# Moving three conversion steps behind a unit boundary, dropping a scatter's wait for a fill, and shifting the first batch's means by a step

## The chip, the cores and the metric

The kernel runs on one core of a Trainium2 chip. The metric is the device time of one launch in microseconds (us). The core has five engines with instruction streams of their own: TensorE (PE, whose weight loads are listed as PEld), VectorE (DVE), ScalarE (ACT), GpSimd (POOL) and SyncE (SP), which in this kernel issues nearly all DMA transfers. Each engine works through its stream strictly in order, and an instruction that waits for a semaphore holds back everything behind it on its engine.

## The reference

Three layers follow one another; every tensor is float32 for the kernel's purposes except the last layer's two weights, which arrive as 64-bit floats.

```python
# attention: 2 batches x 8 heads, S=768, D=64, block=32, window=16
k_sum = k.reshape(B, H, nb, block, D).max(axis=3)
v_sum = v.reshape(B, H, nb, block, D).mean(axis=3)
scores_l = where(|i-j| < window, scale * q @ k.T, -1e9)      # local
scores_s = scale * q @ k_sum.T + log(block)                  # 24 block keys
a = softmax(concat([scores_l, scores_s]));  out = a @ concat([v, v_sum])
# top-1 mixture of experts: 1536 tokens, 512 wide, 8 experts, hidden 1024, capacity 384
expert = argmax(x @ w_gate); gate = softmax prob of it
disp[e, pos] = x[i]          # the first `capacity` tokens of each expert
y = relu(disp @ w1[e]) @ w2[e];  out[i] = gate * y[expert, pos]
# dense layer: 512 -> 2048 -> 512
h = x @ w_in;  g = where(h > 0, h, exp(min(h, 0)) - 1);  return g @ w_out
```

## The kernel before

**Attention** (lines 455 to 775) goes in 24 steps `n` (12 query tiles of 128 tokens, two head groups each). Each step makes scores on PE (`stage_s`, L615), the row maximum on DVE (`stage_max`, L627), exponentials on ACT (`stage_exp`, L640), and, some steps later, transposes (`stage_t`, L661, copied out by ACT at L666) and the product with the values (`stage_o`, L675, scaled by DVE at L686). The order is written out by hand: `T_AT`, `O_AT`, the lists `EARLY`, `LATE`, `END`, and a function `late(n)` that adds the loads and side jobs of step `n`.

The block means of the values are made for each batch of 768 tokens: `pair_sum(b, m)` adds two halves of a value tile in place (L567; there are three tiles, m = 0 to 2, held in `w2raw_131`, `133` and `135`), `block_means` multiplies by a constant averaging matrix on PE (L572), all into one bank of PSUM, and `put_first`, `keep_means` and `put_means` copy the 24 rows of means to where the value tiles of the steps expect them (DVE L589, ACT L590 and L577, POOL L580). `put_spread` (L455) writes a constant into half of a query buffer, once per buffer.

**Dispatch.** Each finished token tile is routed (`gate_1` to `gate_6`, L703 to L764: logits, argmax, the token's position in its expert). POOL then scatters the tile's 128 rows to the DRAM table `xdisp` with an indirect DMA (`put`, L775). The table has a region for each expert, and at its end, from `E * REG` on, a region where no token goes; at step 21 SP writes a constant row into that region (`fill`, L904, 128 x 3 rows of 514 numbers). The scatters are declared free of one another by a no-dependence group called "put"; the list `puts` holds them, and the next load of rows (`load_rows`, L216) waits for all in it.

**Units.** The experts' work runs in units of 384 rows. A unit has eight hidden slices `f` of 128: first layer L241, ReLU on ACT (L1269, `hh` L1270), the low part `hl` on DVE (L1271), second layer L275, three slices later (LAG = 3). Every float32 product is made as three products of a high and a low part. ACT makes the high parts of the weights (`wah`, `wbh`, L233 and L286) and DVE the low parts (`wal` L234, `wbl` L287), in slices `c` of 256. `split_x` (part of `prologue(j, 1)`) transposes the unit's rows on PE (L255), then ACT takes the high part `xh` (L256) and DVE the low part `xl` (L257), four pieces each. With these inputs three units run; the first is mixed into the tail of attention.

**Conversions.** The dense layer's weights come as pairs of 128 x 512 blocks of 64-bit floats, and DVE turns each pair to float32 in three steps (L419, L422, L412). The raw pairs go through a ring of two buffers (`raw_160`, `raw_161`). The last step of a pair issues, on SP, the load of the pair two places later (`conv_next`, L378, two transfers of 512 KB). Units 1 and 2 convert five pairs each, 15 steps spread over the slices f = 0 to 6 by `convert_some`. Unit 1's fifth pair is pair 18 (to `wout_108` from `raw_160`), and its end releases the load of pair 22 into the same buffer; unit 2 converts pairs 20, 22, 24, 26 and 28.

At f = 3 and f = 6 of a unit SP also loads the next unit's weights (`NEXT`: three transfers, then four; an eighth, `w2raw_137`, goes at the next unit's start), 512 KB each. A unit starts with that load, `prologue` (unit 2's row split), the store of the unit's identifiers (L1183) and the load of the rows of the unit after it. After the units the dense layer runs in three groups of 512 rows (L1383).

Of the kernel before, what the change touches and what calls it, by code (L numbers as in the profile page):

```python
# [26 lines left out]
E, F = 8, 1024  # L27
FF = 2048
P = 128
# [9 lines left out]
REG = NT + SLOT  # L39
# [55 lines left out]
def moe_chain_kernel(  # L95
# [339 lines left out]
    with ExitStack() as att:  # L435
# [17 lines left out]
        def put_spread(n, g, copy):  # L453
            rows = heads(1 - g)
            copy(QS[n][rows, g], C("spread")[rows].unsqueeze(1).to_broadcast([D, KD, P]))  # L455
# [132 lines left out]
        def put_first(n):  # L588
            nc.vector.tensor_copy(VXS[n][WK:NK, 0, :], VP[WK:NK, :])  # L589
            nc.scalar.copy(VXS[n][WK:NK, 1, :], VP[WK:NK, :])  # L590

        MEANS_AT = ({2: [1], 3: [2], 4: [3]}, {13: [(2, 0)], 14: [(2, 1)], 15: [(3, 0)], 16: [(3, 1)]})

        OPS = BANK[4].rearrange("p (g u d) -> p g u d", g=2, u=4)
        GPS = BANK[6][:, 0:256].rearrange("p (g n) -> p g n", g=2)
# [73 lines left out]
        def stage_o(i, g):  # L669
            es = st.pop(("t", i, g))  # L670
            vx = vx_of(i)
            op = OPS[:, g]
            for u in range(4):
                for j in range(2):
                    nc.tensor.matmul(  # L675
                        op[j * TQ : (j + 1) * TQ, u, :],
                        es[:, u, j * TQ : (j + 1) * TQ],
                        vx[:, j, (2 * u + g) * D : (2 * u + g + 1) * D],
                        start=True,
                        stop=True,  # L680
                    )
            if g:
                xts[i] = a3.tile([P, ROW], F32, tag="xr", name="xr", bufs=6)
                xt = xts[i][:, 0:DM].rearrange("p (u g d) -> p g u d", g=2, d=D)
                rd = st.pop(("rd", i))
                nc.vector.tensor_tensor(xt, OPS, rd.to_broadcast([P, 2, 4, D]), op=ALU.mult)  # L686
                fill_in()
# [185 lines left out]
        def late(n):  # L873
# [15 lines left out]
                nc.vector.memset(ones_f, 1.0)  # L889
            if n == 1:  # L890
                for g in range(2):
                    put_spread(2, g, nc.gpsimd.tensor_copy)
                nc.gpsimd.memset(fill_row, 0.0)
            if n == 3:
                nc.gpsimd.tensor_copy(fill_row[:, DM:], C("oob")[:, 0:2])
# [5 lines left out]
                load_k(1, 0 if n == 1 else 2, 2)  # L901
            if n == 21:
                nc.sync.dma_start(ids.rearrange("(p a) o -> p (a o)", a=REG // P), oobs)
                nc.sync.dma_start(xdisp[E * REG :, :].rearrange("(s p) d -> p s d", p=P), fill)  # L904
            if n == 0:
                load_q(2)
            if n % 2 == 1 and (n + 5) // 2 < NTT:
# [74 lines left out]
        for n in range(NST - 1):  # L982
            at = lambda lag: steps[n - lag] if 0 <= n - lag < NST else None
            stage_s(*at(0))
            if n == 3:
                stage_o(0, 0)
            for m in T_AT.get(n, ()):
                stage_t(*steps[m])
                stage_e(*steps[m])
            for gate, i in EARLY.get(n, ()):  # L990
                gate(i)
            if at(2) and at(2)[1]:
                st["early"] = early_o(at(2)[0])
            stage_max(*at(0))
            stage_exp(*at(0))
            if n == 2:
                for m in (1, 2):
                    block_means(0, m, 0, last=(m == 2))
            if n == 2:
                put_first(0)  # L1000
                keep_means()
            for slot in MEANS_AT[0].get(n, ()):
                put_means(slot)
            if n == 1:
                block_means(0, 0, 0, first=True)
                block_means(0, 0, 1)
                stage_t(*at(1))
                stage_e(*at(1))
                for m in (1, 2):
                    pair_sum(0, m, nc.vector)  # L1010
            for m in O_AT.get(n, ()):
                stage_o(*steps[m])
            for gate, i in LATE.get(n, []) + END.get(n, []):
                gate(i)
            late(n)
# [154 lines left out]
    def convert_some(j, f):  # L1170

        if j < len(CONV_UNIT):
            n = (CONVS[j + 1] - CONVS[j]) // 2
            todo = [step for m in range(n) for step in conversion(ORDER[CONVS[j] // 2 + m])]
            lo, hi = (min(m, NF1 - 1) * len(todo) // (NF1 - 1) for m in (f, f + 1))
            for step in todo[lo:hi]:
                step()

    def expert_of(j, queue=nc.sync):
        return queue.value_load(listed(0, j), min_val=0, max_val=E - 1)  # L1180
# [67 lines left out]
    def unit(j, expert, finish):  # L1248

        if j > 1:  # L1250
            load_w(expert, NEXT[2])
            for n in range(j == 2, 2):
                prologue(j, n)
        base = nc.sync.value_load(listed(2, j), min_val=0, max_val=NT)
        if j + 1 < MAXU:
            branch_ahead(f"units{j}", n_units > j + 1)
# [55 lines left out]
    def units(j, expert, finish):  # L1312
        if j:
            expert, finish = unit(j, expert, finish)
        if j + 1 < MAXU:
            with tc.If(n_units > j + 1, label=f"units{j}") as more:
                units(j + 1, expert, finish)
            with more.Else():
                if j:
                    last_parts()  # L1320
                if j + 1 < len(CONV_UNIT):
                    for n in range(CONVS[j + 1], NCHUNK - CONV_LATE, 2):
                        convert(ORDER[n // 2])
        else:
            last_parts()
# [228 lines left out]
```

## Time and profile before

| what | value |
|---|---|
| three runs | 420.69, 422.80, 423.19 us (median 422.8) |
| profiled execution | 421.81 us, of it span 419.7 us |
| PE busy | 398.4 us (95% of the span) |
| DVE busy | 336.1 us (80%) |
| ACT busy | 234.7 us (56%) |
| POOL busy | 64.8 us (15%) |
| DMA | 63.60 MB, mean 152 GB/s |
| granted clock of TensorE, mean | 0.993 of full speed |

The profiled execution took 421.81 us, 2.1 us more than its span, and lies 1.0 us under the median of the three runs. Busy shares are means over stages with different limits, so the argument reads stretches of the trace: about 0 to 95 us is attention with the first unit's loads, 95 to 112 us the end of routing, 112 to 210 us the units, and then the dense layer. In a row of the timeline the bracket gives the time that the engine stood idle just before the instruction and what released it.

### The profile page before, as it was taken

The page shows a single profiled execution, that of the slowest core. Times are in us where ns is not written, and L with a number is a line of the kernel's source. Part 1 is how long each engine was busy: PE and PEld are TensorE (multiplying, and loading weights), DVE is VectorE, ACT ScalarE, POOL GpSimd, SP SyncE. Part 2 cuts the span into 40 slices and gives each one's busy share as a digit, 9 for nine tenths or more (in the row PEclk, how much of TensorE's full clock was granted, in tenths as well). Part 3 has the DMA queues.
Part 4 walks back from the last instruction along what each step waited for, and adds up shares of the span by engine and source line. Part 5 has one row for each costly group of instructions (what it writes and reads, how often), then busy time and mean ns, then how long its engine had stood idle before and what let it go on. Part 6 is the DMA issues. An engine that isn't in the chain of part 4 may idle for free.

```text
span 419.7 us, 7891 instructions
## 1 busy us (share of the span) xinstructions
PE 398.4 (95%) x2736; PEld 349.1 (83%) x2736; DVE 336.1 (80%) x675; ACT 234.7 (56%) x586; POOL 64.8 (15%) x129
## 2 busy tenths in 40 slices
PE   7999999989999999799999999999999999999994
PEld 4577677667898989799989889998989898989883
DVE  6789787686589988788879999997788777778870
ACT  4687697762565737166497578645343435343421
POOL 5334776515300000000000000002000002000002
PEclk9999999999999999899999999999999999999998
DMA  8999999699476786985577000202000200100002
GB/s 245 256 285 263 270 275 280 188 345 364 155 228 226 244 301 232 332 255 209 171 271 274 0 2 1 77 0 77 0 0 2 76 2 35 40 2 0 2 2 77
DMA packets 33691, 63.60 MB, mean 152 GB/s; under 512 B 5302, under 2 KB 16191, under 8 KB 33642
## 3 DMA queue, kind: packets, MB, share of 16 engines
q1 hardware_dynamic: 31962, 58.28, 44.9%
q0 software_dynamic: 1680, 4.73, 3.1%
q8 instruction: 23, 0.38, 0.4%
q14 instruction: 26, 0.21, 0.1%
HBM read 50.19 MB, written 13.40 MB: 152 GB/s over the span
## 4 chain that ended last, share of the span: by engine, by line
PE 48%; issue 19%; DVE 16%; DMA 7%; ACT 6%; POOL 1%; SPq 1%; DVEq 0%; another core or an unknown queue 0%; ACTq 0%; POOLq 0%
PE bank L241 21%; PE bank L1383 13%; PE bank L275 5%; DMA half<-in_q_dram 3%; PE bank L661 2%; PE bank L615 2%; ACT ex L640 2%; DMA w2raw<-in_v_dram 2%; PE bank L675 2%; DMA rows<-in_k_dram 2%; DMA raw<-in_moe_w_out_dram 1%; DVE wal L234 1%; DVE win L422 1%; DVE win L412 1%; DVE xrow L1445 1%
## 5 line engine op out<-in xcount | busy, mean ns | idle before, releaser
L1383 PE MATMUL bank<-wout_r,hh 128*128 128x512 f32 x144 | 56.6, 393 | 1.0 <-DVE wout_r L1363 1.0
L640 ACT ACTIVATE ex<-bank,nm 128x120 f32<-128x120 f32 x96 | 33.5, 370 | 9.9 <-DVE nm L627 9.9
L1430 ACT ACTIVATE cst<-bank 128x384 f32<-128x384 f32 x24 | 11.8, 490 | 39.2 <-PE bank L241 39.2
L1430 ACT ACTIVATE xrow<-bank 128x384 f32<-128x384 f32 x24 | 11.7, 489 | 38.4 <-PE bank L241 38.2
L1383 PEld LDWEIGHTS bank<-wout_r,hh 128*128 128x128 f32 x144 | 27.1, 188 | 5.9 <-DVE wout_r L1363 1.7
L1395 POOL DMA_INDIRECT out_dram<-ysb,idt x3 | 2.9, 973 | 178.8 <-DVE xrow L1446 178.2
L1383 PE MATMUL bank<-w2raw_r,hl 128*128 128x512 f32 x72 | 28.7, 399 | 0.5 <-DVE hl L1411 0.5
L1383 PE MATMUL bank<-w2raw_r,hh 128*128 128x512 f32 x72 | 28.2, 392 | 0.0
L241 PE MATMUL bank<-yh,win_r 128*128 128x384 f32 x128 | 27.0, 338 | 0.0
L615 PE MATMUL bank<-kw,half 128*64 128x120 f32 x384 | 24.7, 271 | 1.4 <-DMA half<-in_q_dram 1.4
L1395 POOL DMA_INDIRECT out_dram<-raw,idt x6 | 6.1, 1024 | 119.3 <-ACT raw L1392 118.1
L615 PEld LDWEIGHTS bank<-kw,half 128*64 128x64 f32 x384 | 19.7, 136 | 5.7 <-issue 5.1
L241 PE MATMUL bank<-xh,wal 128*128 128x384 f32 x104 | 23.4, 347 | 0.6 <-DVE wal L234 0.6
L241 PEld LDWEIGHTS bank<-yh,win_r 128*128 128x128 f32 x128 | 22.8, 188 | 0.3
L275 PE MATMUL bank<-hh,wbh_r 128*128 128x384 f32 x96 | 21.1, 341 | 0.0
L1445 DVE SCALAR_TENSOR_TENSOR xrow<-xrow 128x384 f32<-128x384 f32 x24 | 13.3, 556 | 9.2 <-ACT xrow L1432 8.5
L640 ACT ACTIVATION_READ_ACCUMULATOR ex<-bank,nm 128x1 f32 x96 | 20.6, 215 | 0.0
L275 PE MATMUL bank<-hl,wbh_r 128*128 128x384 f32 x96 | 20.6, 336 | 0.0
L1445 DVE SCALAR_TENSOR_TENSOR xrow<-cst,xrow 128x384 f32<-128x384 f32 x24 | 13.3, 556 | 8.6 <-ACT cst L1432 8.6
L241 PEld LDWEIGHTS bank<-xh,wal 128*128 128x128 f32 x104 | 18.7, 193 | 1.8 <-DVE wal L234 1.6
L661 PE MATMUL bank<-cst,ex 128*120 128x128 f32 x96 | 17.2, 289 | 0.7 <-ACT ex L640 0.5
L666 ACT COPY es<-bank 120x512 f32<-120x512 f32 x24 | 14.2, 593 | 6.3 <-PE bank L661 4.4
(286 smaller groups left out, 1108.0 us busy)
## 6 DMA issues: line engine op xcount, KB each, us to landing
raw<-in_moe_w_out_dram SPq DMA_DIRECT2D x16, 512.0 KB
w1raw<-in_moe_w_dram SPq DMA_DIRECT2D x12, 512.0 KB
w2raw<-in_moe_w_dram SPq DMA_DIRECT2D x12, 512.0 KB
raw<-in_moe_w_in_dram SPq DMA_DIRECT2D x10, 512.0 KB
half<-in_q_dram SPq DMA_DIRECT2D x24, 128.0 KB
w2raw<-in_v_dram SPq DMA_DIRECT2D x6, 512.0 KB
rows<-in_moe_w_in_dram SPq DMA_DIRECT2D x6, 512.0 KB
yr<-ydT SPq DMA_DIRECT2D x4, 768.0 KB
```

The lines of the kernel that those rows point to most:

```text
L234: nc.vector.tensor_tensor(lo, src, hi.bitcast(F32), op=ALU.subtract)
L241: nc.tensor.matmul(hp, wa[a][:, kk, cols], xa[b][:, kk, :], start=(n == kk == 0), stop=(n == 2 and kk == KD - 1))
L275: nc.tensor.matmul(ACC[d][:, 0:SLOT], wb[a][:, jj, d * P : (d + 1) * P], hb[b], start=(f == 0 and n == 0), stop=(f == NF1 - 1 and n == 2),)
L615: nc.tensor.matmul(sp[cols, u, :], qts[i][:, g, u, cols], kws[i][:, g, u, j, :], start=True, stop=True)
L640: nc.scalar.activation(ex[:, u, :], sp[:, u, :], AF.Exp, bias=nm[:, u : u + 1], accum_out=dens[i][:, g, u])
L661: nc.tensor.transpose(ep[:, u, :], ex[:, u, :], ident)
L666: nc.scalar.copy(es, st.pop(("e", i, g)))
L675: nc.tensor.matmul(op[j * TQ : (j + 1) * TQ, u, :], es[:, u, j * TQ : (j + 1) * TQ], vx[:, j, (2 * u + g) * D : (2 * u + g + 1) * D], star ...
L1383: nc.tensor.matmul(ACC[s], ga[a][:, cols], wb[b][:, jj, :], start=(f == n == 0), stop=(f == NF2 - 1 and n == 2),)
L1395: put = nc.gpsimd.indirect_dma_start(out, bass.IndirectOffsetOnAxis(ap=IDT[g % 3][:, s : s + 1], axis=0), OBS[(NS * g + s) % len(OBS)], No ...
L1430: nc.scalar.activation(x, hp, AF.Relu, scale=-1.0)
L1445: nc.vector.scalar_tensor_tensor(z, x, 1.0, z, op0=ALU.add, op1=ALU.mult)
```

## The change

Four edits. (1) The first batch's last pair sum (tile m = 2) moves on DVE from the end of step 1 to step 2, behind that step's maximum; its PE product moves behind step 3's scores, and the copies of the means (`put_first`, `keep_means`, the `put_means` slots) move a step later; `stage_o(0, 0)` follows them to the end of step 3's exponentials. (2) Two `put_spread` copies at step 1 move from POOL to ACT. (3) The fill's store joins the group "put" and the list `puts`. (4) In unit 1, the conversion steps that stood at f = 6 (the three steps of pair 18) are kept back and issued after unit 2's `prologue`, or in the other branch where there is no unit 2.

```diff
--- before.py
+++ after.py
@@ -589,7 +589,7 @@
             nc.vector.tensor_copy(VXS[n][WK:NK, 0, :], VP[WK:NK, :])
             nc.scalar.copy(VXS[n][WK:NK, 1, :], VP[WK:NK, :])
 
-        MEANS_AT = ({2: [1], 3: [2], 4: [3]}, {13: [(2, 0)], 14: [(2, 1)], 15: [(3, 0)], 16: [(3, 1)]})
+        MEANS_AT = ({3: [1], 4: [2], 5: [3]}, {13: [(2, 0)], 14: [(2, 1)], 15: [(3, 0)], 16: [(3, 1)]})
 
         OPS = BANK[4].rearrange("p (g u d) -> p g u d", g=2, u=4)
         GPS = BANK[6][:, 0:256].rearrange("p (g n) -> p g n", g=2)
@@ -889,7 +889,7 @@
                 nc.vector.memset(ones_f, 1.0)
             if n == 1:
                 for g in range(2):
-                    put_spread(2, g, nc.gpsimd.tensor_copy)
+                    put_spread(2, g, nc.scalar.copy)
                 nc.gpsimd.memset(fill_row, 0.0)
             if n == 3:
                 nc.gpsimd.tensor_copy(fill_row[:, DM:], C("oob")[:, 0:2])
@@ -901,7 +901,10 @@
                 load_k(1, 0 if n == 1 else 2, 2)
             if n == 21:
                 nc.sync.dma_start(ids.rearrange("(p a) o -> p (a o)", a=REG // P), oobs)
-                nc.sync.dma_start(xdisp[E * REG :, :].rearrange("(s p) d -> p s d", p=P), fill)
+                spare = nc.sync.dma_start(xdisp[E * REG :, :].rearrange("(s p) d -> p s d", p=P), fill).ins
+                tc.declare_no_dep(spare, group="put", reason="no token has a row there")
+                tc.add_to_no_dep_group("put", spare)
+                puts.append(spare)
             if n == 0:
                 load_q(2)
             if n % 2 == 1 and (n + 5) // 2 < NTT:
@@ -983,7 +986,7 @@
             at = lambda lag: steps[n - lag] if 0 <= n - lag < NST else None
             stage_s(*at(0))
             if n == 3:
-                stage_o(0, 0)
+                block_means(0, 2, 0, last=True)
             for m in T_AT.get(n, ()):
                 stage_t(*steps[m])
                 stage_e(*steps[m])
@@ -992,13 +995,16 @@
             if at(2) and at(2)[1]:
                 st["early"] = early_o(at(2)[0])
             stage_max(*at(0))
+            if n == 2:
+                pair_sum(0, 2, nc.vector)
+            if n == 3:
+                put_first(0)
             stage_exp(*at(0))
             if n == 2:
-                for m in (1, 2):
-                    block_means(0, m, 0, last=(m == 2))
-            if n == 2:
-                put_first(0)
+                block_means(0, 1, 0)
+            if n == 3:
                 keep_means()
+                stage_o(0, 0)
             for slot in MEANS_AT[0].get(n, ()):
                 put_means(slot)
             if n == 1:
@@ -1006,8 +1012,7 @@
                 block_means(0, 0, 1)
                 stage_t(*at(1))
                 stage_e(*at(1))
-                for m in (1, 2):
-                    pair_sum(0, m, nc.vector)
+                pair_sum(0, 1, nc.vector)
             for m in O_AT.get(n, ()):
                 stage_o(*steps[m])
             for gate, i in LATE.get(n, []) + END.get(n, []):
@@ -1173,8 +1178,17 @@
             n = (CONVS[j + 1] - CONVS[j]) // 2
             todo = [step for m in range(n) for step in conversion(ORDER[CONVS[j] // 2 + m])]
             lo, hi = (min(m, NF1 - 1) * len(todo) // (NF1 - 1) for m in (f, f + 1))
-            for step in todo[lo:hi]:
-                step()
+            if j == 1 and f == NF1 - 2:
+                put_off.extend(todo[lo:])
+            elif j != 1 or not put_off:
+                for step in todo[lo:hi]:
+                    step()
+
+    put_off = []
+
+    def convert_rest():
+        for step in put_off:
+            step()
 
     def expert_of(j, queue=nc.sync):
         return queue.value_load(listed(0, j), min_val=0, max_val=E - 1)
@@ -1251,6 +1265,8 @@
             load_w(expert, NEXT[2])
             for n in range(j == 2, 2):
                 prologue(j, n)
+            if j == 2:
+                convert_rest()
         base = nc.sync.value_load(listed(2, j), min_val=0, max_val=NT)
         if j + 1 < MAXU:
             branch_ahead(f"units{j}", n_units > j + 1)
@@ -1316,6 +1332,8 @@
             with tc.If(n_units > j + 1, label=f"units{j}") as more:
                 units(j + 1, expert, finish)
             with more.Else():
+                if j == 1:
+                    convert_rest()
                 if j:
                     last_parts()
                 if j + 1 < len(CONV_UNIT):
```

DVE at the boundary of unit 1 and unit 2 (`hl_156` and `hl_1901` belong to unit 1's slices f = 6 and 7, `wal_141` and `xl_93` to unit 2). Before:

```order
L1271 TENSOR_TENSOR hl_156<-cst,hh_155 128x384
L419 TENSOR_SCALAR wout_108<-raw_160 128x1024
L422 SCALAR_TENSOR_TENSOR wout_108<-raw_160,wout_108 128x1024
L412 SCALAR_TENSOR_TENSOR wout_108<-raw_160,wout_108 128x1024
L287 TENSOR_TENSOR wbl_r<-w2raw_137,wbh_r 128x1024
L234 TENSOR_TENSOR wal_141<-w1raw_123,wah_r 128x1024
L1271 TENSOR_TENSOR hl_1901<-cst,hh_1900 128x384
L257 TENSOR_TENSOR xl_93<-bank_84,xh_92 128x384
L257 TENSOR_TENSOR xl_93<-bank_91,xh_92 128x384
L234 TENSOR_TENSOR wal_143<-w1raw_125,wah_142 128x1024
```

After the change:

```order
L1287 TENSOR_TENSOR hl_156<-cst,hh_155 128x384
L287 TENSOR_TENSOR wbl_r<-w2raw_137,wbh_r 128x1024
L234 TENSOR_TENSOR wal_141<-w1raw_123,wah_r 128x1024
L1287 TENSOR_TENSOR hl_1901<-cst,hh_1900 128x384
L257 TENSOR_TENSOR xl_93<-bank_84,xh_92 128x384
L257 TENSOR_TENSOR xl_93<-bank_91,xh_92 128x384
L419 TENSOR_SCALAR wout_108<-raw_160 128x1024
L422 SCALAR_TENSOR_TENSOR wout_108<-raw_160,wout_108 128x1024
L412 SCALAR_TENSOR_TENSOR wout_108<-raw_160,wout_108 128x1024
L234 TENSOR_TENSOR wal_143<-w1raw_125,wah_142 128x1024
```

Pair 18's three steps have moved from ahead of seven instructions (`wbl_r`, `wal_141`, `hl_1901` and the four `xl`, of which two are shown) to behind them. Line 1271 is now 1287.

SP at the same boundary, with the semaphores that each row waits for (`DMAHW` ones count landed transfers). The first two rows load pair 20, the `raw_160` rows load pair 22. Before:

```order
L378 DMA raw_161<-in_moe_w_out_dram 128x512 [waits DMAHW5_49,DVE_49]
L378 DMA raw_161<-in_moe_w_out_dram 128x512 [waits DMAHW6_49]
L378 DMA raw_160<-in_moe_w_out_dram 128x512 [waits DMAHW2_49,DVE_49]
L378 DMA raw_160<-in_moe_w_out_dram 128x512 [waits DMAHW7_49,DMAHW3_49]
L201 DMA w2raw_133<-in_moe_w_dram 128x2x512 [waits DMAHW0_49,Activation_49]
L205 DMA w1raw_127<-in_moe_w_dram 128x4x256 [waits DMAHW1_49]
L205 DMA w1raw_129<-in_moe_w_dram 128x4x256 [waits Activation_49]
L201 DMA w2raw_135<-in_moe_w_dram 128x2x512 [waits Activation_49]
L201 DMA w2raw_137<-in_moe_w_dram 128x2x512 [waits DMAHW0_49,DVE_49,Activation_49]
```

After the change:

```order
L378 DMA raw_161<-in_moe_w_out_dram 128x512 [waits DMAHW5_49,DVE_49]
L378 DMA raw_161<-in_moe_w_out_dram 128x512 [waits DMAHW6_49]
L201 DMA w2raw_133<-in_moe_w_dram 128x2x512 [waits Activation_49]
L205 DMA w1raw_127<-in_moe_w_dram 128x4x256 [waits DMAHW7_49]
L205 DMA w1raw_129<-in_moe_w_dram 128x4x256 [waits DMAHW0_49,Activation_49]
L201 DMA w2raw_135<-in_moe_w_dram 128x2x512 [waits DMAHW1_49,Activation_49]
L201 DMA w2raw_137<-in_moe_w_dram 128x2x512 [waits DMAHW6_49,DVE_49,Activation_49]
L378 DMA raw_160<-in_moe_w_out_dram 128x512 [waits DMAHW7_49,DMAHW2_49,DVE_49]
L378 DMA raw_160<-in_moe_w_out_dram 128x512 [waits DMAHW3_49,DMAHW0_49]
```

The load of pair 22 has moved behind five weight loads of 512 KB, and its two halves now also wait for semaphores (`DMAHW7`, `DMAHW0`) that two of these weight loads use; the weight loads no longer stand behind it.

POOL at the scatter of token tile 7, with what each row waits for. Before:

```order
L757 TENSOR_SCALAR row<-r 128x1
L759 TENSOR_SCALAR ob<-rank,cap 128x1 [waits DVE_49]
L764 TENSOR_SCALAR idx<-row,ob 128x1 [waits Pool_49]
L775 DMA xdisp<-xr,idx 15744x514 [waits DMAHW2_49,DMAHW3_49,DMAHW1_49,DMAHW5_49,Activation_49,Pool_49]
L723 COPY xr<-cst 128x1 [waits DMASW2_49]
L757 TENSOR_SCALAR row<-r 128x1 [waits DVE_49]
```

After the change:

```order
L757 TENSOR_SCALAR row<-r 128x1
L759 TENSOR_SCALAR ob<-rank,cap 128x1 [waits DVE_49]
L764 TENSOR_SCALAR idx<-row,ob 128x1 [waits Pool_49]
L775 DMA xdisp<-xr,idx 15744x514 [waits DMAHW2_49,DMAHW1_49,DMAHW3_49,Activation_49,Pool_49]
L723 COPY xr<-cst 128x1 [waits DMASW2_49]
L757 TENSOR_SCALAR row<-r 128x1 [waits DVE_49]
```

The scatter has lost one of its waits, that for `DMAHW5`, the semaphore of the fill's store. `DMAHW1` to `DMAHW3` are the three row loads of the first unit.

## Rows read from the trace of the kernel before

**Rows 1.** Busy by stretch: PE, PEld, DVE, ACT, POOL, clock, DMA share, GB/s.
```profile
180.00:200.00 20.00, 20.00 (x117) 20.00 (x116) 17.31 (x22) 12.45 (x22) 0.00 (x0) 1.00 0.73 245
```

**Rows 2.** Timeline of DVE, 162 to 204: start, duration, operation, idle before.
```profile
164.28 0.69 DVE L419 TENSOR_SCALAR wout<-raw 128x1024 uint32<-128x1024 uint32 x1 [1.44 <-DMA raw<-in_moe_w_out_dram]
...
167.41 1.22 DVE L287 TENSOR_TENSOR wbl_r<-w2raw,wbh_r 128x1024 fp32r<-128x1024 f32 x1
...
170.15 1.94 DVE L257 TENSOR_TENSOR xl<-bank,xh 128x384 fp32r<-128x384 f32 x4
...
181.55 0.69 DVE L419 TENSOR_SCALAR wout<-raw 128x1024 uint32<-128x1024 uint32 x1
...
203.60 1.22 DVE L287 TENSOR_TENSOR wbl_r<-w2raw,wbh_r 128x1024 fp32r<-128x1024 f32 x1
```

**Rows 3.** Timeline of SP's DMA issues, 157 to 176.
```profile
157.79 0.83 SPq L378 DMA_DIRECT2D raw<-in_moe_w_out_dram  x2
...
162.40 0.80 SPq L378 DMA_DIRECT2D raw<-in_moe_w_out_dram  x2
...
167.53 0.81 SPq L378 DMA_DIRECT2D raw<-in_moe_w_out_dram  x2
...
169.29 0.40 SPq L201 DMA_DIRECT2D w2raw<-in_moe_w_dram  x1
...
175.11 0.39 SPq L201 DMA_DIRECT2D w2raw<-in_moe_w_dram  x1
```

**Rows 4.** Timeline of PE at unit 2's start and its last low products.
```profile
170.76 1.11 PE L241 MATMUL bank<-xh,wah_r 128*128 128x384 f32 x4 [2.61 <-DVE xl L257]
...
206.49 0.85 PE L275 MATMUL bank<-hh,wbl_r 128*128 128x384 f32 x4
```

**Rows 5.** Timeline of ACT, the high parts of unit 2's rows.
```profile
165.01 1.66 ACT L256 CAST xh<-bank 128x384 fp32r<-128x384 f32 x4 [0.22 <-PE bank L255]
```

**Rows 6.** Busy by stretch, columns as in rows 1.
```profile
170.00:172.00 2.00, 1.24 (x6) 1.24 (x7) 2.00 (x5) 0.00 (x0) 0.00 (x0) 0.85 1.01 396
172.00:174.00 2.00, 2.00 (x8) 2.00 (x7) 1.23 (x2) 0.00 (x0) 0.00 (x0) 0.50 1.04 354
174.00:176.00 2.00, 2.00 (x11) 2.00 (x10) 0.47 (x1) 1.50 (x3) 0.00 (x0) 0.79 1.08 372
```

**Rows 7.** Waits of DVE, 171 to 210: us in total, times, longest.
```profile
DVE hl L1271 <- ACT hh L1270: 3.2, 2, 2.3
```

**Rows 8.** Timeline of SP: the fill's store.
```profile
86.87 0.61 SPq L904 DMA_DIRECT2D xdisp<-fill_row  x1
```

**Rows 9.** Timeline of POOL, 84 to 98.
```profile
84.61 0.73 POOL L764 TENSOR_SCALAR idx<-row,ob 128x1 uint32<-128x1 f32 x1
97.76 1.10 POOL L775 DMA_INDIRECT xdisp<-xr,idx  x1 [12.43 <-ACT wbl L705]
```

**Rows 10.** DMA of the stretch 84 to 98.
```profile
DMA packets 1837, 4.87 MB, mean 348 GB/s; under 512 B 283, under 2 KB 283, under 8 KB 1835
```

**Rows 11.** Timeline of DVE, 99 to 109.
```profile
99.37 0.16 DVE L732 TENSOR_REDUCE r<-vv 128x1 f32<-128x8 f32 x1 [1.76 <-POOL row L757]
...
108.76 0.15 DVE L1096 TENSOR_TENSOR prod<-am,cst 32x2 f32<-32x2 f32 x1 [0.98 <-issue]
```

**Rows 12.** Timeline of PE, 99 to 110.
```profile
99.86 0.18 PE L750 MATMUL bank<-oh,tri_b 128*128 128x8 bf16 x1 [0.89 <-DVE oh L734]
...
109.69 0.28 PE L1107 MATMUL bank<-prod,ones_f 32*1 32x72 f32 x2 [0.84 <-DVE prod L1101]
```

**Rows 13.** Timeline of DVE, the pair sum of tile 2.
```profile
17.51 0.69 DVE L567 TENSOR_TENSOR w2raw<-w2raw 128x512 f32<-128x512 f32 x1 [1.58 <-DMA w2raw<-in_v_dram]
```

**Rows 14.** Timeline of ACT, 16 to 20.
```profile
16.60 1.12 ACT L666 COPY es<-bank 120x512 f32<-120x512 f32 x2
19.70 0.36 ACT L640 ACTIVATE ex<-bank,nm 128x120 f32<-128x120 f32 x1 [1.97 <-DVE nm L627]
```

**Rows 15.** Timeline of PE, the scores that follow a query load.
```profile
39.04 1.04 PE L615 MATMUL bank<-kw,half 128*64 128x120 f32 x16 [1.05 <-DMA half<-in_q_dram]
```

## The prediction

> **What bounds the kernel now.** I read the page's busy shares first, then the table by stretches, then the timelines of DVE, PE, POOL and SP where PE stands idle. In the units PE is the bound: between 180 and 200 us it is busy for 20.00 of 20 us at full clock, DVE for 17.31 [rows 1]. So an edit is worth what it takes out of PE's idle places, and only if DVE, with some 13% to spare, can follow. The reader should see three idle places that the edits speak to: 2.61 us at the start of unit 2 [rows 4], 0.89 and 0.84 us at the end of routing [rows 12], and at the beginning a DVE stall [rows 13] that comes long before PE's next wait for a transfer [rows 15].
>
> **Conversions moved behind unit 2's start.** DVE stands 1.44 us for pair 18's raw data (issued at 157.79 [rows 3]) and then works on it from 164.28 to 167.41 [rows 2], 3.13 us. Behind that, in order, stand `wbl_r`, `wal`, `hl` and the four `xl`, which begin at 170.15; PE's first product of unit 2 waits for the first `xl` and has stood 2.61 us [rows 4]. With the three steps gone from there, everything behind moves up by 1.44 + 3.13 = 4.57 us: the `xl` run from 165.58 to 167.52. ACT's `xh` are no bound, since the four lie between 165.01 and 166.67 [rows 5]. PE finishes its work before the gap at 170.76 - 2.61 = 168.15, so the `xl` are there 0.6 us before PE asks: the 2.61 us go.
>
> After the gap the granted clock reads 0.85, 0.50 and 0.79 in three stretches of 2 us [rows 6], though PE was idle only at the start of the first. Work lost to it: 2 x (0.15 + 0.50 + 0.21) = 1.72 us. Ahead of the gap and from 180 on it is 1.00 [rows 1]. If the fall comes from the gap, it goes with it, and the edit is worth 2.61 + 1.72 = 4.33 us; if it does not, 2.61. I take 4.33, because nothing else near 170 differs from the stretches with full clock.
>
> Is that gain kept to the end of the unit? Now pair 18's 3.13 us lie ahead of unit 2's own work on DVE. DVE began the unit's work 4.57 us earlier and PE 4.33, so against PE it has 4.57 - 4.33 - 3.13 = 2.89 us less. Against that stand DVE's own idle time in the unit, 3.2 us waiting for ACT's `hh` [rows 7], most of it while the clock is low, and a margin at the end: `wbl_r` ends at 203.60 + 1.22 = 204.82 and PE uses it at 206.49 [rows 2, 4], 1.67 us. Together 4.87 against 2.89, so about 2 us of slack. I cost it at nothing; without that cover it would be up to 2.89 us.
>
> **Its transfers.** SP is in order too. Before, it stood at pair 22's load until pair 18 was converted (167.53), and the weight loads followed from 169.29 [rows 3]. Now it passes from pair 20's load (162.40) straight to the four weight loads, so I expect these at about 164, 5 us earlier; nobody waits for them yet. The fifth, `w2raw_137`, waits for a landed load: before it was issued at 175.11 [rows 3], 5.8 us after 169.29, so now at about 170. Pair 22's two halves come behind it, the first not before pair 18's end (167.52 + 3.13 = 170.65), the second when one more weight load has landed, about 1.4 us later by 512 KB at 372 GB/s [rows 6], near 172. Pair 18 took 164.28 - 157.79 = 6.5 us from issue to use [rows 3, 2]; so pair 22 is there between 177 and 178.5. Its first step ran at 181.55 [rows 2] and would run at 181.55 - 4.33 = 177.2. It comes in time or up to 1.3 us late, inside the 2 us of slack: nothing, at most 1.3 us.
>
> The Trainium skill (DMA: Bandwidth & Descriptors, Anatomy of one DMA) gives, for transfers that GpSimd issues, about 2.0 us plus bytes over 436 GB/s, so 4.4 us for a pair of 1 MB, an estimate. The trace disagrees, with 6.5 us under a busy queue, and by the page the 1.44 us stall would hardly be there and pair 22 would be early; the measured time is the one used above.
>
> **Fill store out of the scatters' way.** Tile 7's index is ready at 84.61 + 0.73 = 85.34 and its scatter starts at 97.76, after 12.43 us [rows 9]. The view puts that on an ACT copy (`wbl`, L705), but it belongs to a later tile; of the waits of this scatter in the order above, the one that lasts is that for the fill, issued at 86.87 [rows 8] behind megabytes of raw loads. POOL is in order, so routing of the next tiles stands behind it: DVE waits 1.76 us for a POOL instruction and PE 0.89 us for DVE; at the end DVE stands 0.98 us, where POOL clears `prod` behind its last scatters, and PE 0.84 us [rows 11, 12]. With the scatter free at 85.34 I take both PE gaps away: 0.89 + 0.84 = 1.73 us. Bounds: 0, if other waits take their place, and 1.76 + 0.98 = 2.74, if DVE is the bound there. 1.73 is what PE, the engine that carries the time onward, shows. The unit's loads hang on the lists made at the end of this chain, so they move up with it. The fill itself has nobody behind it but the next load of rows, some 20 us later.
>
> **The beginning.** The pair sum no longer holds DVE 1.58 us for its tile [rows 13]. Against that, ACT gets two `put_spread` copies between the two `es` copies; at the 0.56 us of one `es` copy [rows 14] these are 1.12 us, and ACT stands idle 1.97 us right behind [rows 14]. The means' copies come a step later, as does their product. Gain at most 1.58, loss at most 1.12. But at 39.04 PE waits 1.05 us for a query tile [rows 15]: what is won ahead of it is waited out there, and a loss of up to 1.05 disappears there too. I take 0; what gets past lies between a loss of 0.07 and, if the query's load moves up as well, a gain of 1.58.
>
> **Sum.** 4.33 + 1.73 + 0 = 6.06 us. Against the profiled 421.81 that gives 415.75, against the median of 422.8, which is 1.0 higher, 416.7; against the mean of the four known times (422.1) 416.1, which I forecast. Bounds by the terms: 422.1 - (4.33 + 2.74 + 1.58) = 413.5 and 422.1 - 2.61 + 0.07 = 419.6.
>
> **Rivals.** (a) Pair 22 or 24 comes late and DVE loses more than its 2 us in unit 2. For it: DMA is at a full share from 170 to 176 [rows 6], five weight loads lie ahead, and the second half waits for a landing. Against it: these loads start 5 us earlier. PE then waits 1 to 2 us near the end of the unit: 417.1 to 418.1.
>
> (b) The fill edit buys nothing: the scatter's last wait was another, or DVE, near its limit behind routing, does not pass the gain on. For it: the view names ACT. Against it: that copy stands behind this scatter in the program. 416.1 + 1.73 = 417.8.
>
> (c) The scatters that are now free at 85 to 97 take DMA time from the loads that the first unit waits for. Three of them, 128 x 514 x 4 bytes each, are 0.79 MB, 2.3 us at the stretch's 348 GB/s [rows 10]; if DVE waits that long for its raw pair or rows, the 1.73 us are gone and 0.6 more: 418.4. Against it: the same bytes were written right behind, and the engines' work only changes places. The Trainium skill (DMA: Bandwidth & Descriptors, Queues, rings and completion order) says that a DMA engine takes packets of the queues it serves in turn, by which the scatters would not queue behind SP's loads but halve them while they last; the trace shows a total of 348 GB/s, not the turns.
>
> (d) Slower: the wait that pair 18 had returns with each of the four later pairs, since the ring now runs one step late through unit 2: 4 x 1.44 = 5.76 us on DVE, less its slack of 2 us, is 3.76 us of PE idle in two gaps, each with a fall of the clock like the present one, 2 x 1.72. That is 7.2 lost against 6.06 won: 423.2. It decides from 1.16 us of wait a pair on (4 x 1.16 - 2 + 3.44 = 6.08). Against it: unit 1 had this wait once, at its last pair.
>
> (e) The clock fall stays: 416.1 + 1.72 = 417.8.
>
> **Chances.** Forecast 0.60; (a) 0.13; (b) 0.10; (c) 0.06; (d) 0.05; (e) 0.06. Faster and slower by over 1% mean under 418.6 and over 427.0, about what a measurement of this kernel can tell from no change. (a), (b), (c) and (e) lie just under that line, so a third of their 0.35 and a little of the forecast's falls over it: faster 0.73, same 0.23, slower 0.04 for what is in no list. The range 413.8 to 419.6 leaves out (d) and the tails.
>
> **What would show it.** In the profile of the changed kernel: no idle time before unit 2's first L241 and a clock of 1.00 in the stretches after it; no wait of DVE for raw data at pair 18; pair 22's first step without a DMA wait, or with one under 2 us and PE still unbroken to the unit's end; the weight loads at about 164 instead of 169; tile 7's scatter right behind its index near 85, no wait of DVE for POOL near 99 and none at `prod`; and at step 10 PE's query wait longer by what the beginning won. Wrong would be a new idle place of PE in unit 2, a DVE wait for raw data around 92 or in each pair, or a clock still at 0.50 after the boundary.

## The result and the profile after

The changed kernel takes 417.72 us (median of six runs, 416.47 to 418.91) against 422.51 us (median of six, 420.69 to 423.22): a ratio of 0.9894, 95% interval 0.9866 to 0.9921, so 4.5 us (3.3 to 5.7) faster. The forecast was 416.1 and 6.1 us. The profiled execution has a span of 417.0 us; it was the slowest of the six. The ratios, here and below, leave out an execution that took over 1.5% more than the fastest of its kernel, one each of e5, e8 and e11 below; in e8 and e11 it is the profiled one, so their traces are not read here.

The idle places at the end of routing and at unit 2's start are gone. POOL, DVE and PE of the changed kernel, against [rows 9, 11, 4]; lines 1096 and 1271 are now 1101 and 1287:

```profile
86.24 1.10 POOL L775 DMA_INDIRECT xdisp<-xr,idx  x1 [0.28 <-POOL idx L764]
```
```profile
98.34 0.16 DVE L732 TENSOR_REDUCE r<-vv 128x1 f32<-128x8 f32 x1
...
107.43 0.15 DVE L1101 TENSOR_TENSOR prod<-am,cst 32x2 f32<-32x2 f32 x1
```
```profile
166.75 0.85 PE L241 MATMUL bank<-xh,wah_r 128*128 128x384 f32 x4
```

Tile 7's scatter starts right behind its index, DVE has no bracket (no idle time) at either place, and PE goes into unit 2 without a gap. The stretches of [rows 6], clock in the third column from the right, all read 1.00:

```profile
170.00:172.00 2.00, 2.00 (x14) 2.00 (x13) 1.97 (x4) 1.02 (x2) 0.00 (x0) 1.00 1.06 378
172.00:174.00 2.00, 2.00 (x13) 2.00 (x12) 1.96 (x2) 0.78 (x2) 0.00 (x0) 1.00 1.04 381
174.00:176.00 2.00, 2.00 (x14) 2.00 (x13) 1.69 (x2) 1.45 (x5) 0.00 (x0) 1.00 0.84 338
```

What is new stands later in unit 2. DVE waits for raw data twice, ACT waits for DVE's `gate` with a weight cast behind it, and PE waits for ACT and DVE (the last row's 0.97 us are not new: the same wait stood at 219.69 with 0.98 before):

```profile
174.74 1.22 DVE L412 SCALAR_TENSOR_TENSOR wout<-raw,wout 128x1024 uint32<-128x1024 uint32 x1
177.22 0.69 DVE L419 TENSOR_SCALAR wout<-raw 128x1024 uint32<-128x1024 uint32 x1 [1.26 <-DMA raw<-in_moe_w_out_dram]
...
186.49 0.70 DVE L419 TENSOR_SCALAR wout<-raw 128x1024 uint32<-128x1024 uint32 x1 [2.98 <-DMA raw<-in_moe_w_out_dram]
...
188.56 0.17 DVE L264 RECIPROCAL gate<-gate 128x3 f32<-128x3 f32 x1
```
```profile
188.77 0.72 ACT L269 ACTIVATE xrow<-xrow,gate 128x512 f32<-128x512 f32 x1 [8.26 <-DVE gate L264]
189.40 1.03 ACT L233 CAST wah<-w1raw 128x1024 fp32r<-128x1024 f32 x1
```
```profile
190.48 0.97 PE L241 MATMUL bank<-xh,wah 128*128 128x384 f32 x4 [0.65 <-ACT wah L233]
191.74 0.96 PE L241 MATMUL bank<-xh,wal 128*128 128x384 f32 x4 [0.29 <-DVE wal L234]
202.81 0.97 PE L275 MATMUL bank<-hh,wbl_r 128*128 128x384 f32 x4 [0.33 <-DVE wbl_r L287]
208.02 0.96 PE L241 MATMUL bank<-yh,wal 128*128 128x384 f32 x4 [0.74 <-DVEq L1516]
217.12 0.50 PE L1401 MATMUL bank<-wout_r,hh 128*128 128x512 f32 x1 [0.97 <-DVE wout_r L1381]
```

The row at 174 is the last step of pair 20, which frees the buffer for pair 24; those at 177 and 186 are the first steps of pairs 22 and 24. On SP, pair 22 goes out at 170.73 in two halves that take 1.7 us, and the identifiers, the row loads and pair 24 stand behind it:

```profile
162.86 0.40 SPq L201 DMA_DIRECT2D w2raw<-in_moe_w_dram  x1
...
170.73 1.72 SPq L378 DMA_DIRECT2D raw<-in_moe_w_out_dram  x2
173.52 0.33 SPq L1197 DMA_DIRECT2D ids<-it  x1
176.35 1.57 SPq L216 DMA_DIRECT2D xrow<-xdisp  x3
178.03 0.84 SPq L378 DMA_DIRECT2D raw<-in_moe_w_out_dram  x2
```

Before, DVE at pairs 20 and 24, and SP's load of pair 24:

```profile
180.42 1.22 DVE L412 SCALAR_TENSOR_TENSOR wout<-raw,wout 128x1024 uint32<-128x1024 uint32 x1
...
188.67 0.69 DVE L419 TENSOR_SCALAR wout<-raw 128x1024 uint32<-128x1024 uint32 x1
```
```profile
181.66 0.82 SPq L378 DMA_DIRECT2D raw<-in_moe_w_out_dram  x2
```

There pair 24 went out as soon as pair 20 was done (181.64), and DVE used it 7.0 us later without a wait. After the change pair 20 was done at 175.96, but SP was at the row loads until 177.92: pair 24 went out 2.1 us after pair 20's end and was used 8.5 us later, while DVE asked for it 7.5 us after that end (186.49 - 2.98 = 183.51).

PE's milestones, each against the same instruction before, give the account of the two profiled executions (minus is earlier):

| place | before | after | difference |
|---|---|---|---|
| L615, the query wait of [rows 15] | 39.04 | 38.24 | -0.80 |
| L482, behind the last attention steps | 88.70 | 89.33 | +0.63 |
| L255, unit 1's rows transposed, behind routing and unit 0 | 128.11 | 126.89 | -1.22 |
| L241, unit 2, slice 0 | 170.76 | 166.75 | -4.01 |
| L241, unit 2, slice 1 | 176.59 | 170.91 | -5.68 |
| L241, dense layer's first | 209.99 | 206.42 | -3.57 |
| first L1383 (now L1401) | 219.69 | 217.12 | -2.57 |

So 0.80 us were won up to 39 us, routing gave 1.85, the gap 2.79 and the clock 1.67; 1.43 were lost in attention between 39 and 89 us, and 3.11 from unit 2's second slice to 217 us. That is 2.57 us between two single executions; the medians lie 4.8 apart, because the one profiled before was 0.7 under its median and the one after 1.2 over it.

### The profile page after: what moved, and what is told of

The parts are those of the page before. It is cut to its first block, busy times and chain, and to the rows that moved or that the text cites. A ratio compares the mean times of both kernels' runs of the same rounds, so it can differ in the third digit from the quotient of the medians.

```text
span 417.0 us, 7891 instructions
## 1 busy us (share of the span) xinstructions
PE 398.1 (95%) x2736; PEld 348.5 (84%) x2736; DVE 334.5 (80%) x675; ACT 236.1 (57%) x588; POOL 64.6 (15%) x127
## 5 line engine op out<-in xcount | busy, mean ns | idle before, releaser
L1401 PE MATMUL bank<-wout_r,hh 128*128 128x512 f32 x144 | 56.6, 393 | 1.0 <-DVE wout_r L1381 1.0
L1401 PEld LDWEIGHTS bank<-wout_r,hh 128*128 128x128 f32 x144 | 27.1, 188 | 6.0 <-DVE wout_r L1381 1.7
L1401 PE MATMUL bank<-w2raw_r,hl 128*128 128x512 f32 x72 | 28.8, 399 | 0.5 <-DVE hl L1429 0.5
L1401 PE MATMUL bank<-w2raw_r,hh 128*128 128x512 f32 x72 | 28.2, 392 | 0.0
L241 PE MATMUL bank<-yh,win_r 128*128 128x384 f32 x128 | 27.0, 337 | 0.0
L615 PE MATMUL bank<-kw,half 128*64 128x120 f32 x384 | 25.4, 276 | 1.2 <-DMA half<-in_q_dram 0.9
L615 PEld LDWEIGHTS bank<-kw,half 128*64 128x64 f32 x384 | 20.3, 140 | 5.6 <-issue 4.0
L241 PE MATMUL bank<-xh,wal 128*128 128x384 f32 x104 | 22.9, 341 | 0.9 <-DVE wal L234 0.9
L241 PEld LDWEIGHTS bank<-yh,win_r 128*128 128x128 f32 x128 | 22.8, 188 | 0.3
L241 PEld LDWEIGHTS bank<-xh,wal 128*128 128x128 f32 x104 | 18.1, 188 | 2.4 <-DVE wal L234 2.2
L627 DVE TENSOR_REDUCE nm<-bank 128x4 f32<-128x480 f32 x24 | 15.6, 652 | 4.5 <-PE bank L615 3.6
```

The costliest lines, as they stand in the source:

```text
L241: nc.tensor.matmul(hp, wa[a][:, kk, cols], xa[b][:, kk, :], start=(n == kk == 0), stop=(n == 2 and kk == KD - 1))
L615: nc.tensor.matmul(sp[cols, u, :], qts[i][:, g, u, cols], kws[i][:, g, u, j, :], start=True, stop=True)
L627: nc.vector.tensor_reduce(nm, sp, axis=AX.X, op=ALU.max, negate=True)
L1401: nc.tensor.matmul(ACC[s], ga[a][:, cols], wb[b][:, jj, :], start=(f == n == 0), stop=(f == NF2 - 1 and n == 2),)
```

## The experiments

Each ratio is to the kernel before, run on the same chip in the same job.

**The parts alone.** The diffs are the parts of the one shown above.

```diff
 e1: only put_off / convert_rest
 e2: only the fill's store in group "put" and in puts
 e3: only pair_sum, block_means, put_first, keep_means, MEANS_AT, put_spread
 e4: e1 and e2 together
```

Conversions alone. 

> Only pair 18's three conversion steps are moved behind unit 2's start. My theory (the boundary pays what was forecast, then two later pairs come late): no PE idle time before unit 2's first product and a clock of 1.00 there, 4.4 us won at that place; then DVE waits for pair 24 by 2 to 3 us, ACT's row scaling and weight cast stand behind it, and PE loses 2.5 to 3.2 us up to the dense layer's first product, so the whole is 1.2 to 2 us faster than before (ratio 0.995 to 0.997). Rival (the late pair is an accident of the one profiled run of the full change): 4.4 us faster, ratio 0.9895.

Fill alone. 

> Only the fill's store is made free of the scatters. My theory: tile 7's scatter starts within 1.5 us of its index near 86 instead of 98, the DVE wait for POOL near 99 and the PE gaps of 0.89 and 0.84 us are gone, 1.8 us faster (ratio 0.9957). Rival (other waits take their place, or the freed scatters delay the raw loads of that stretch): the scatter starts early but the time is the same within 0.5 us, with a new DVE wait for raw data near 93.

Beginning alone. 

> Only the edits at the beginning (pair sum, means, two copies on ACT). My theory by the traces: 0.8 us ahead at 40 to 70 us, as in the full change; whether it is kept is open. If the wait of ACT at 72.3 and the clock fall to 0.50 after it belong to these edits, this run shows them again and is 0.5 to 0.7 us slower than before at 97 us, ratio 1.000 to 1.003. Rival (that stall was chance in one run): 0.8 us ahead is kept, ratio 0.998.

Conversions and fill. 

> The conversions and the fill without the edits at the beginning. My theory: the sum of the two parts, 3.0 to 4.0 us faster than before (ratio 0.9905 to 0.993); against the full change it differs by less than 1 us. If the beginning's edits carry gain of their own this one is 0.8 us slower than the full change; if they cause the stall near 73 it is 0.6 us faster in its profile at 97 us.

| kernel | ratio | interval |
|---|---|---|
| e1 conversions | 0.9954 | 0.9925 to 0.9983 |
| e2 fill | 0.9972 | 0.9942 to 1.0002 |
| e3 beginning | 1.0009 | 0.9990 to 1.0029 |
| e4 conversions, fill | 0.9924 | 0.9893 to 0.9955 |

The conversions alone are worth 1.9 us, not 4.4: the late pair is no accident. The product of e1 and e2, 0.9926, is e4, and the beginning's edits are worth nothing measurable. In e1 the fill still holds the scatter, and here the view names it; pair 24 is late by 3.12 us:

```profile
98.67 1.10 POOL L775 DMA_INDIRECT xdisp<-xr,idx  x1 [12.09 <-DMA xdisp<-fill_row]
```
```profile
188.48 0.69 DVE L419 TENSOR_SCALAR wout<-raw 128x1024 uint32<-128x1024 uint32 x1 [3.12 <-DMA raw<-in_moe_w_out_dram]
```

In e2 the scatter is free (86.86), PE's two routing gaps are gone, and PE is 0.6 us ahead at 156 us. But pair 18's data do not come earlier, so DVE waits longer for them and PE's gap at unit 2 grows from 2.61 to 3.22: the gain is waited out there in its profile, and only 1.2 us are measured, with an interval that reaches no change.

```profile
164.29 0.70 DVE L419 TENSOR_SCALAR wout<-raw 128x1024 uint32<-128x1024 uint32 x1 [2.04 <-DMA raw<-in_moe_w_out_dram]
```
```profile
170.76 1.65 PE L241 MATMUL bank<-xh,wah_r 128*128 128x384 f32 x4 [3.22 <-DVE xl L257]
```

In e3 PE is 0.75 us ahead at 88 us and 1.73 at unit 2's start. The clock did not fall after the gap this time, and then, with no conversion moved, pair 24 is late all the same. The stall near 73 us is not there, so it does not belong to these edits. PE, the stretch behind the gap, and DVE of e3:

```profile
169.03 0.96 PE L241 MATMUL bank<-xh,wah_r 128*128 128x384 f32 x4 [2.57 <-DVE xl L257]
...
192.76 0.96 PE L241 MATMUL bank<-xh,wah 128*128 128x384 f32 x4 [0.54 <-ACT wah L233]
```
```profile
170.00:172.00 2.00, 2.00 (x13) 2.00 (x13) 1.50 (x2) 0.55 (x2) 0.00 (x0) 1.00 1.02 264
```
```profile
188.76 0.70 DVE L419 TENSOR_SCALAR wout<-raw 128x1024 uint32<-128x1024 uint32 x1 [3.31 <-DMA raw<-in_moe_w_out_dram]
```

In e3 pair 22's load stands where it stood before, ahead of the weight loads, and pair 24 still goes out 1.4 us after pair 20's end, behind the row loads, and is used 9.0 us later. So pair 24 is the next limit of unit 2 whatever lets the unit run faster; in the three profiles of kernels with the gap in which the clock fell (before, e2 and e12 below) it is late by 0, 0 and 0.39 us.

**The full change again, and three ways at the late pair.**

The full change. 

> The changed kernel as it is, again. My theory: pair 24 late by about 3 us in DVE's first step of it, PE's waits in unit 2 of 0.65, 0.29 and 0.33 us and one of 0.3 to 0.75 at the dense layer, ACT's es copy near 73 late by 0.7 us; all of these again, since they are set by the order; the clock fall to 0.50 after 74 us may or may not come again. Ratio 0.989 to 0.992. Rival (the late pair is chance): no DVE wait over 1 us for pair 24, and a time near 415.

It gave 0.9911 (0.9875 to 0.9947), with waits of 0.95 and 2.85 us for pairs 22 and 24. PE's waits stand at the same four places, with 0.21, 0.28, 0.41 and 0.42 us (0.65, 0.29, 0.33 and 0.74 after). PE's idle time near 76 was 0.44 this time, with a clock of 1.00 from 70 to 82 us, so the stall at 73 and the fall after it are not set by the order. In this execution the clock fell elsewhere, to 0.55 and 0.60 from 60 to 64 us, behind a wait of PE of 0.94 us at 58.

```profile
178.62 0.69 DVE L419 TENSOR_SCALAR wout<-raw 128x1024 uint32<-128x1024 uint32 x1 [0.95 <-DMA raw<-in_moe_w_out_dram]
...
187.77 0.69 DVE L419 TENSOR_SCALAR wout<-raw 128x1024 uint32<-128x1024 uint32 x1 [2.85 <-DMA raw<-in_moe_w_out_dram]
```

```diff
 e6:
+            if f in ROWS_AT and j + 1 < MAXU:
+                scale_x(XROW, [ROWS_AT.index(f)])
             convert_some(j, f)
 ...
-            if f in ROWS_AT and j + 1 < MAXU:
-                scale_x(XROW, [ROWS_AT.index(f)])
```

The row scaling first. 

> The full change, and in a unit the row scaling of the next unit's rows is issued ahead of the slice's conversion steps, so that DVE's gate does not stand behind pair 24's first step and ACT's weight cast does not stand behind the gate. My theory (the late pair reaches PE through ACT, which waits for the gate): PE's waits of 0.65 and 0.29 us near 190 and their after-effects (1.5 us) are gone, DVE's wait for pair 24 stays 2 to 3 us, those near 203 and 208 (0.6 and 1.0 us) shrink or stay: 1 to 2 us faster than the full change, ratio 0.985 to 0.988. Rival (DVE itself is late, and PE waits for its wal anyway): the same as the full change within 0.3 us.

0.9829 (0.9783 to 0.9875): 414.52 us, 3.5 us better than the full change in the same job (0.9829 / 0.9911), more than the 1 to 2 us expected. Pair 24 is still 2.35 us late, but ACT now waits 3.11 us for the gate (8.26 in the profile after), its cast runs while DVE still waits for the pair, and PE has no idle time in unit 2 up to the dense layer's first products:

```profile
181.09 0.72 ACT L269 ACTIVATE xrow<-xrow,gate 128x512 f32<-128x512 f32 x1 [3.11 <-DVE gate L264]
181.72 1.03 ACT L233 CAST wah<-w1raw 128x1024 fp32r<-128x1024 f32 x1
```
```profile
183.40 0.69 DVE L419 TENSOR_SCALAR wout<-raw 128x1024 uint32<-128x1024 uint32 x1 [2.35 <-DMA raw<-in_moe_w_out_dram]
```
```profile
202.99 0.97 PE L241 MATMUL bank<-yh,wal 128*128 128x384 f32 x4 [0.35 <-DVEq L1516]
```

That confirms the chain from the pair through the gate and ACT to PE. But not all of the 3.5 us are the late pair's. From unit 2's first product to the dense layer's wait at L1401, e5's profile takes 49.70 us and e6's 47.87: 1.83 less. Another 1.25 are won in unit 1 (from the L255 of the table to unit 2's first product, 39.90 and 38.65), where no pair was late and ACT's cast stood behind the same scaling. These two waits of the profile after, which the kernel before has too, are gone in e6:

```profile
153.73 0.97 PE L241 MATMUL bank<-xh,wah 128*128 128x384 f32 x4 [0.40 <-ACT wah L233]
154.99 0.97 PE L241 MATMUL bank<-xh,wal 128*128 128x384 f32 x4 [0.29 <-DVE wal L234]
```

```diff
 e7: evict() of unit 1 keeps its base; in unit 2, behind convert_some(j, f) of f = 2:
+            if j == 2 and f == LAG - 1:
+                store(kept.pop())
 e8: in conv_load
+            queue = nc.gpsimd if i in (22, 24, 26, 28) else nc.sync
```

The store later. 

> The full change, and the store of unit 1's results (768 KB) is issued behind pair 26's load instead of between pair 24's and pair 26's. My theory (pair 24's load shares the queue with that store and lands 8.4 us after issue, where pair 18 took 6.5): it lands 1.5 to 2.5 us sooner, DVE's wait for it falls from 3.0 to 0.5 to 1.5 us, PE's waits near 190 fall to 0.3 or nothing, 1 to 2 us faster than the full change. Rival (it is late because it is issued late, behind the row loads): landing and wait unchanged.

0.9883 (0.9846 to 0.9920), 1.2 us better than the full change by the medians, which the intervals don't tell apart. Pair 24, issued at 179.43, was used at 187.04, 7.6 us, where the full change needed 8.3 to 8.5; the wait fell to 2.15 us, less than expected. By this one profile the store is a part of the lateness, not its main cause.

```profile
179.43 0.85 SPq L378 DMA_DIRECT2D raw<-in_moe_w_out_dram  x2
```
```profile
187.04 0.69 DVE L419 TENSOR_SCALAR wout<-raw 128x1024 uint32<-128x1024 uint32 x1 [2.15 <-DMA raw<-in_moe_w_out_dram]
```

POOL's queue. 

> The full change, with the loads of pairs 22, 24, 26 and 28 issued by POOL, which is idle in the units, instead of SP. My theory (pairs 22 and 24 are late because SP issues them behind weight and row loads): pair 24 is issued at the end of pair 20's conversion near 176 instead of 178, pair 22 without waiting for the landed weight loads, DVE waits under 1 us for either, 1.5 to 3 us faster than the full change. Rival (POOL's own issuing takes long, or the queues share the engines so that the landing is as late): DVE waits of 2 to 3 us stay and the time is that of the full change or slower.

0.9953 (0.9921 to 0.9985), by the ratios 1.8 us slower than the full change, which the intervals don't tell apart. The 1.5 to 3 us that the theory wanted are not there, as the rival has it; which of the rival's two reasons holds is not shown.

**Combinations.**

```diff
 e9:  e6 and e7 together
 e10: e6, and load_w(expert, NEXT[2]) behind convert_rest()
 e11: e6's edit in the kernel before;  e12: the kernel before
```

Scaling and store. 

> Both: the row scaling ahead of the conversion steps, and the store of unit 1's results behind pair 26's load. My theory: with the scaling ahead PE no longer waits in unit 2 for the late pair, so the later store has little left to give: 0 to 0.5 us on the version with the scaling alone, ratio 0.980 to 0.984. Rival (the late pair still costs PE time at the unit's end through DVE's wbl): 1 us or more faster than that version.

Scaling and weight load. 

> The row scaling ahead of the conversion steps, and the weight load w2raw_137 issued behind pair 22's load instead of ahead of it. My theory: pair 22 no longer waits for w2raw_133 to land and is there 1 to 1.5 us sooner, DVE's wait for it (1.05 us) goes, and the time is that of the version with the scaling alone within 0.5 us, since PE stands nowhere for it. Rival (DVE is the bound of unit 2): 1 us faster.

Scaling alone. 

> The kernel before, with only the row scaling ahead of the conversion steps in the units. My theory: the units 1 and 2 lose their PE waits behind ACT's weight cast (0.39 and 0.29 us in unit 1, and in unit 2 where it runs at full clock), and the gap of 2.6 us at unit 2's start stays: 0.7 to 2 us faster than before (ratio 0.995 to 0.998), so that the three edits are worth 5 to 6 us with this scaling against 3 to 4.5 without. Rival (the scaling was worth its 3.4 us by itself): ratio 0.992.

The kernel before again. 

> The kernel before once more, for its profile. My theory: the gap of about 2.6 us at unit 2's start is there again, since the order sets it; whether the clock falls behind it is open (it fell in the profiles of before and of the fill alone, not in that of the beginning's edits alone). If it falls, pair 24 is waited for by under 0.5 us and PE has no wait near 190; if it does not, pair 24 is waited for by 2.5 to 3.5 us and PE has waits of 0.5 and 0.3 us near 192. Rival (the two have nothing to do with each other): clock fall and a wait over 2 us for pair 24 together, or neither.

e9 gave 0.9806 (0.9752 to 0.9860), e10 0.9804 (0.9758 to 0.9850), 413.02 us and the best of all, 9 us under the kernel before; from e6 neither is told apart. In e10 pair 22 is there in time, as expected, and pair 24 is still late, which PE no longer feels; so pair 22's late second half is not what makes pair 24 late:

```profile
171.88 0.69 DVE L419 TENSOR_SCALAR wout<-raw 128x1024 uint32<-128x1024 uint32 x1
...
182.22 0.69 DVE L419 TENSOR_SCALAR wout<-raw 128x1024 uint32<-128x1024 uint32 x1 [2.86 <-DMA raw<-in_moe_w_out_dram]
```

e11 gave 0.9956 (0.9923 to 0.9989), 1.9 us: the scaling is no 3.4 us by itself, but about half of it has nothing to do with the change. With it the change is worth 0.9829 / 0.9956 = 0.987, 5.4 us; without it 0.9894 and 0.9911, some 4.1 us. The 1.3 us between them have the sign that the late pair's cost should have (1.8 us in the two profiles above), but the intervals of these ratios are wider, so the times alone do not show it.

e12's profile has the gap again (2.86 us), the clock falls, and pair 24 is late by only 0.39 us, as the theory wants where the clock falls; PE has no wait near 190. It is a single execution:

```profile
170.84 1.65 PE L241 MATMUL bank<-xh,wah_r 128*128 128x384 f32 x4 [2.86 <-DVE xl L257]
```
```profile
170.00:172.00 2.00, 1.16 (x4) 1.16 (x5) 2.00 (x5) 0.00 (x0) 0.00 (x0) 0.61 1.00 369
172.00:174.00 2.00, 2.00 (x8) 2.00 (x7) 1.31 (x2) 0.00 (x0) 0.00 (x0) 0.53 0.90 309
```
```profile
189.03 0.69 DVE L419 TENSOR_SCALAR wout<-raw 128x1024 uint32<-128x1024 uint32 x1 [0.39 <-DMA raw<-in_moe_w_out_dram]
```

## Why the prediction came out as it did

The direction and the places were right, and the time lies in the range; the forecast promised 6.1 us and 4.5 were there.

- **The gap and the clock** were 2.79 and 1.67 us against 2.61 and 1.72. That the fall belongs to the gap is shown as far as this: no profile without the gap has a fall there, and of the profiles with it (before, e2, e3, e12) e3's alone has none.
- **"I cost it at nothing"** is the step that failed. It tested DVE's slack at the unit's end and the arrival of pair 22, which was 1.26 us late, within the bounds given. The slack itself was counted rightly: DVE's waits for `hh` fell from 3.2 to 0.30 us, by the 2.89 that the sum takes from them. But it did not follow SP's queue one pair further: pair 24 goes out behind the row loads, 2.1 us after its buffer is free, takes 8.5 us to its use and came 2.98 us late. (Pair 22's new place is not the cause: in e3, without it, and in e10, with pair 22 in time, pair 24 is 3.31 and 2.86 us late.) DVE waited 4.24 us, not up to 1.3, against a slack of 2. Nor did it ask who waits for DVE besides PE: ACT's scaling waits for the gate, and the next weights' cast stands behind it. That is rival (a), which had 1 to 2 us and a chance of 0.13; it cost 3.1 us in the profile and 2.4 in e5's of the same kernel (again from unit 2's second slice to L1401, against the profile before). The measured 417.7 lies where that rival put it, at 417.1 to 418.1. Of the 3.5 us of e6 against e5, 1.8 fall in unit 2, and the rest is not the late pair's.
- **The fill** was right in mechanism; the size (1.85 in the profile for 1.73) was partly luck. From L482 to L255 of the table the profiles with a free fill read here take 37.54 to 37.56 us, and those without it 39.41 (before), 39.08 (e1), 38.51 (e12) and 38.45 (e3): 0.9 to 1.9 us more. The forecast was read from the one that showed most; in e12, the same kernel again, PE has the wait of 0.85 at 109.51 and none near 99. Alone the fill is worth 1.2 us, with an interval that reaches no change. In its profile 0.6 us are waited out at unit 2, where pair 18's load went out 0.6 us earlier and was used at the same time; in e3, with PE 1.7 us ahead, that load did come 1.7 earlier, so this loss is not shown to be the rule.
- **The beginning**: 0 was forecast on the ground that the query wait at 39.04 takes up any gain. That ground did not hold in the profile after. The query came earlier too, the case that the forecast had named as its upper bound: PE's wait there was 0.92 instead of 1.05, and 0.8 us were kept to 68 us. Whether the edits did that is open: with them that row stands anywhere from 37.01 (e10) to 40.09 (e7), without them from 38.94 to 39.81. The end effect was none (e3: 1.0009). In e3's profile the lead is lost in unit 2, where pair 24 is late; that this is so in its other executions is not shown.
- **Attention's loss** of 1.43 us in the profile after is in no term. ACT's `es` copy at 72.32 started 0.7 us later behind its matmuls than in the profile before, PE stood 1.16 us, and the clock fell behind it (0.87, 0.50 and 0.78 from 74 to 80). Three of the profiles (after, e1, e4) have that stall and the others read for it don't, e5 of the same kernel among them; its cause stays open, and the clock fell behind it in one of the three. A loss of this size needs no cause in the edits: over seven profiles whose attention is the same as that of the changed kernel (after, e3, e5, e6, e7, e9, e10), the L482 of the table stands anywhere from 86.56 to 91.02 us.

## What to carry to other kernels

A wait that is removed moves the whole stage forward, and its transfers need not come along by as much (here DVE asked for pair 24 5.2 us earlier and it went out 3.6 earlier): look up each later load that the stage consumes, with everything that stands ahead of it in its issuing queue, and compare its landing with the new time of need. Ask of an engine with slack not only whether it keeps up, but which short result other engines take from it: here a 0.17 us reciprocal behind a late conversion held up a weight cast on ACT and PE. Putting such a result ahead of the work that may wait gave 3.5 us here, some 1.8 of them where the pair was late, though the pair stayed late; of the two ways to hurry the data, the store behind it gave 1.2 us and the other queue none, and neither is clear of the noise.

## What was not expected of the hardware

The granted clock does not answer each gap alike: after PE's gaps of 2.61, 2.86 and 3.22 us at one place the lowest stretch of 2 us read 0.50, 0.53 and 0.54 (1.00 is 2.4 GHz, the upper of its two levels, and 0.50 the lower), after one of 2.57 us it stayed at 1.00, after gaps of about 1.15 us near 74 it fell once in three times, and in e5 it fell to 0.55 behind one of 0.94 us at 58. And a load of 1 MB that DVE waited for took 6.5 to 7.1 us from issue to use when it was pair 18 and 7.5 to 9.1 when it was pair 24, which goes out behind 0.8 MB of row loads; where DVE did not wait for pair 24 (before, e2) it was there within 7.0 and 7.1. The Trainium skill (DMA: Bandwidth & Descriptors, Anatomy of one DMA) has 4.4 us for that size by its formula for GpSimd's transfers, an estimate which none of these loads reached.
